# One layout of a DRAM copy, one more chunk pair in seven products, and a new order, in an attention and softplus-MLP kernel

## The chip, the cores and the metric

The kernel runs on one core of a Trainium2 chip. The metric is device microseconds of one execution; three executions of the kernel before give the median used here. One more execution was recorded by the hardware profiler, and every row shown below comes from that one.

## The reference

```python
# x: (8, 8, 512, 64) = batch B, head H, position S, D;  state: (8, 8, 32, 64)
scores = scale * np.matmul(x, state.transpose(0, 1, 3, 2))
a = softmax(scores)
xread = np.matmul(a, state)                                # (B, H, 512, 64)
scores2 = scale * np.matmul(state, x.transpose(0, 1, 3, 2))
sread = np.matmul(softmax(scores2), x)                     # (B, H, 32, 64)
attn = np.concatenate([xread, sread], axis=2)
x = attn.transpose(0, 2, 1, 3).reshape(8 * 544, 512)       # 4352 rows
h = x @ w_in                                               # 512 -> 2048
g = np.maximum(h, 0.0) + np.log1p(np.exp(-np.abs(h)))      # softplus
return (g @ w_out).astype(np.float32)                      # 2048 -> 512
```

## The kernel before, in words

Every float32 operand of a large product is held as two parts, a rounded high part and the remainder, in one double tile of 128 partitions by 2 x 512 words (4 KB a partition, 512 KB in all), and a product is three passes: high by high, high by low, low by high (`PASSES`). ScalarE writes the high part (L288), VectorE the low part (L304); `split` makes both operations.

For the positions of a batch the kernel doesn't form xread. It multiplies the states by `w_in` first: `V.{b}.{c}.{g}` holds, for batch b, column block c (four blocks of 512) and head parity g, the product of 4 heads' 32 states with their rows of `w_in`, 128 rows by 512, as high and low. The hidden block is then `h.{b}.{f} = V^T a` (L307), six wide matmuls with the softmax weights `a.{b}.{g}`, for 16 blocks f of 128. Batches 0 to 3 get their V from TensorE batch by batch (`B.V...`). Batches 4 to 7 (`STACKED`) get theirs together: for each block c, head pair q and parity o one product `B.K...` gives 128 rows by 512, the 32 states of one head for four batches (`vq`), split into `vt.{c}.{q}.{o}`. There are 32 such tiles. Each is stored to DRAM (`Sv.{c}.{q}.{o}`, the `vd` tensors, L298), and later, for each of the four batches, c and o, the load `Lv.{b}.{c}.{o}` (L295) collects the rows of that batch from the four q into one V tile. What is stored is sorted by batch, and what is loaded is sorted by head.

The second GEMM has two forms. Batches 0 to 2 use `m.{b}.{f}.{c}`, three matmuls of 512 columns each. From batch 3 on (`SWEPT`), half a batch (256 positions, two row blocks) by two blocks of the hidden dimension (u, a chunk pair: blocks 2u and 2u+1) is either a direct product of 12 matmuls of 512 columns (L756), or Strassen-like, seven products of half size, 21 matmuls of 256 columns in four steps (L746). The second form needs four sums of the softplus blocks (`sf`, L728 to L730, split into `gS`) and, once for each u, sums of the weights: `ci0.u`, `ci1.u` (L674) and `cf.u` (L680 to L683), split into `F.u`, `E` and a part of `Wc`. `SWEPT` lists the u that use it: 1 to 7 in ten half batches; (3, 0) has none; batch 8 stands for the 256 state rows.

Weights travel through DRAM too: `W.f`, 16 tiles, are stored by `Sw.f` to `wd` and come back as `Lb.f` for the second half of batch 2 and `Lc.f` from batch 3; the split `w_in` is stored by `Su` and comes back for the state rows (`Lu`). Softmax weights of the state rows pass through `te` (stores `Se`, loads `Le`).

All is placed by hand: `PLAN` is a list of `name:engine:buffers`. It sets the order on each engine, and the SBUF slot (41 double slots) or PSUM bank of each tile. Nearly every DMA is issued from SP, in the list's order; an instruction on SP waits until its data are there and its slot is free, and all behind it wait too. A slot is free when its last reader is done, and for a tile that is stored that reader is the store.

```python
V.b.c.o    = rows (q, n), q head pair, n state, of batch b      # what h reads
vt.c.q.o   = rows (b, n), of head pair q, four batches          # what is stored
```

Of the kernel before, what the change touches and what calls it, by code (L numbers as in the profile page):

```python
# [90 lines left out]
gl.2.0:V: Le.1.0.0:S: e.3.1:A: m.0.15.0:T: H.2.1:V:13 Le.1.0.2:S: gh.2.1:A:35 h.2.4:T:7 Le.1.0.1:S: H.3.1:V:1 s.2.2:A:14 Se.2.1:S: o.0.2.0:V:
Se.3.1:S: Lk.1:S:4 gl.2.1:V: m.2.0.0:T:0 So.0.0:S: m.2.0.1:T:6 s.2.3:A:12 Lk.0:S: s.2.4:A:0 m.2.0.2:T:1 gh.2.2:A:37 m.2.0.3:T:3 gh.2.3:A:8 gl.2.2:V:
B.V3.3+R1:T:2,4,5 gl.2.3:V: uh.0.3:A:22 uh.0.2:A:39 ul.0.3:V: gh.2.4:A:3 ul.0.2:V: Su.0.3:S: m.2.1.0:T: X.1:V:2 vh.3.3.0:A:23 Su.0.2:S: vh.3.3.1:A:34
m.2.1.1:T: vl.3.3.0:V: kh:A:40 vl.3.3.1:V: h.2.5:T:7 kl:V: m.2.1.2:T: s.2.5:A:3 m.2.1.3:T: B.K0.2+K0.3:T:5,2,4,7 gl.2.4:V: uh.1.0:A:27 uh.1.1:A:7
ul.1.0:V: gh.2.5:A:29 ul.1.1:V: Su.1.0:S: m.2.2.0:T: gh.v0.2.0:A:33 Su.1.1:S: gh.v0.2.1:A:17 m.2.2.1:T: gl.v0.2.0:V: gh.v0.3.0:A:25 gl.v0.2.1:V:
h.2.6:T:5 Sv.0.2.0:S: gh.v0.3.1:A:36 gl.v0.3.0:V: Sv.0.2.1:S: gl.v0.3.1:V: Sv.0.3.0:S: m.2.2.2:T: s.2.6:A:9 Sv.0.3.1:S: m.2.2.3:T:
B.K1.0+K1.1:T:2,4,7,5 gl.2.5:V: gh.2.6:A:0 m.2.3.0:T: gh.v1.0.0:A:2 gh.v1.0.1:A:13 m.2.3.1:T: gl.v1.0.0:V: gh.v1.1.0:A:35 gl.v1.0.1:V: h.2.7:T:2
Sv.1.0.0:S: gh.v1.1.1:A:22 gl.v1.1.0:V: Sv.1.0.1:S: gl.v1.1.1:V: Sv.1.1.0:S: m.2.3.2:T: s.2.7:A:14 Sv.1.1.1:S: m.2.3.3:T: gh.2.7:A:39 gl.2.6:V:
B.V3.0+V3.1:T:4,7,5,2 uh.0.0:A:28 uh.0.1:A:37 ul.0.0:V: ul.0.1:V: Su.0.0:S: Su.0.1:S: m.2.4.0:T: vh.3.0.0:A:7 vh.3.0.1:A:27 m.2.4.1:T: vl.3.0.0:V:
vh.3.1.0:A:33 vl.3.0.1:V: h.2.8:T:4 vh.3.1.1:A:17 vl.3.1.0:V: vl.3.1.1:V: m.2.4.2:T: s.2.8:A:13 gl.2.7:V: m.2.4.3:T: Lb.8:S:25 gh.2.8:A:36  # L100
B.K0.0+K0.1:T:7,5,2,4 m.2.5.0:T: gh.v0.0.0:A:4 gh.v0.0.1:A:31 m.2.5.1:T: gl.v0.0.0:V: gh.v0.1.0:A:8 gl.v0.0.1:V: h.2.9:T:7 Sv.0.0.0:S: gh.v0.1.1:A:30
Lb.9:S:6 gl.v0.1.0:V: uh.1.3:A:11 Sv.0.0.1:S: uh.1.2:A:38 gl.v0.1.1:V: Sv.0.1.0:S: m.2.5.2:T: s.2.9:A:12 ul.1.3:V: Sv.0.1.1:S: m.2.5.3:T: gh.2.9:A:2
ul.1.2:V: Su.1.3:S: T.1:T:5 h.2.10:T:2 gl.2.8:V: th.1:A: Su.1.2:S: tl.1:V: gl.2.9:V: m.2.6.0:T: s.2.10:A:1 Lb.10:S:13 m.2.6.1:T: gh.2.10:A:35
m.2.6.2:T: m.2.6.3:T: B.K1.2+K1.3:T:4,7,5,2 m.2.7.0:T: gl.2.10:V: gh.v1.2.0:A:22 gh.v1.2.1:A:3 Lb.11:S:14 m.2.7.1:T: gl.v1.2.0:V: Lz.4:S:7
gh.v1.3.0:A:28 gl.v1.2.1:V: h.2.11:T:4 Sv.1.2.0:S: gh.v1.3.1:A:37 gl.v1.3.0:V: Sv.1.2.1:S: gl.v1.3.1:V: Sv.1.3.0:S: m.2.7.2:T: s.2.11:A:8 Sv.1.3.1:S:
m.2.7.3:T: gh.2.11:A:19 M.3.0:V: h.2.12:T:7 gl.2.11:V: e.3.0:A: Ms.3.0:V: m.2.8.0:T: Lb.12:S:29 m.2.8.1:T: m.3.1:A: H.3.0:V:4 m.2.8.2:T: m.3.0:A:
N.3.1:V: Se.3.0:S: m.2.8.3:T: s.2.12:A:0 h.2.13:T:5 N.3.0:V: Nm.3.1:V: Lb.13:S:1 m.2.9.0:T: gh.2.12:A:4 s.2.13:A:3 Nm.3.0:V: m.2.9.1:T: uh.2.1:A:31
gl.2.12:V: m.2.9.2:T: uh.2.0:A:8 ul.2.1:V: gh.2.13:A:30 m.2.9.3:T: ul.2.0:V: Su.2.1:S: h.2.14:T:2 gl.2.13:V: Su.2.0:S: Lb.14:S:0 D.3.1:V:9 m.2.10.0:T:
D.3.0:V:14 s.2.14:A:2 m.2.10.1:T: gh.2.14:A:24 ah.3.1:A:11 m.2.10.2:T: ah.3.0:A:38 Lc.0:S:5 al.3.1:V: m.2.10.3:T: Lt.4.0:S:10 uh.3.0:A:21 al.3.0:V:
Lt.4.1:S:39 B.K2.0+K2.1:T:4,7,5,2 uh.3.1:A:22 Lc.1:S:3 ul.3.0:V: ul.3.1:V: Su.3.0:S: gl.2.14:V: m.2.11.0:T: Su.3.1:S: gh.v2.0.0:A:28 gh.v2.0.1:A:37  # L110
# [823 lines left out]
```

## Time and profile before

| | us |
|---|---|
| median of 3 executions (773.69 to 774.62) | 774.41 |
| the profiled execution, its own time | 775.73 |
| its span, first to last instruction | 773.9 |
| TensorE busy | 648.2 (84%) |
| VectorE busy | 448.0 (58%) |
| ScalarE busy | 365.9 (47%) |
| DMA engines, mean busy share | 0.45 |

The profiled execution's time is its span and 1.8 us around it. Names in the rows are those of the tiles with the buffer numbers left out: `vd<-vt` is a store `Sv`, `V<-vd` a load `Lv`, `wd<-W` a store `Sw`. PE is TensorE, DVE is VectorE, ACT is ScalarE, and SPq the sequencer that issues DMAs. A line that waits for several things names the one that came last. The DMA share is the mean over the core's 16 DMA engines, so 4 engines at work and 12 idle read as 0.25.

### The profile page before, as it was taken

Reading aid. Unit: us, or ns where it says so; the run is one execution under the profiler, and the core shown is the slowest. Engines: PE = TensorE matmul, PEld = TensorE weight load, DVE = VectorE, ACT = ScalarE, POOL = GpSimd, SP = SyncE. Lnnn points to the kernel's source line nnn. Section 1 sums busy time; section 2 is a strip of 40 time slices with the busy share of each in tenths; the row PEclk is TensorE's granted clock in tenths of the full one; section 3 lists DMA queues with packets and bytes.
Section 4 is the critical chain, followed back from the end, with each engine's and each line's share of the span. In section 5 each row is a group of like instructions: output and inputs, shape, how many; then the busy total and the mean of one; then the engine's idle time right before and its main releaser. Section 6 shows DMA issues by size and latency. Waiting matters only on the chain.

```text
span 773.9 us, 11435 instructions
## 1 busy us (share of the span) xinstructions
PE 648.2 (84%) x4308; PEld 537.6 (69%) x4308; DVE 448.0 (58%) x957; ACT 365.9 (47%) x729; POOL 1.0 (0%) x7
## 2 busy tenths in 40 slices
...
GB/s 354 366 83 100 178 105 65 62 266 380 128 106 187 192 164 272 167 170 122 264 195 125 227 240 110 83 116 188 95 214 148 251 148 30 139 188 118 19 28 28
DMA packets 47191, 124.22 MB, mean 161 GB/s; under 512 B 4896, under 2 KB 14624, under 8 KB 47136
## 3 DMA queue, kind: packets, MB, share of 16 engines
q1 hardware_dynamic: 46992, 122.97, 44.2%
...
q10 hardware_dynamic: 144, 0.52, 0.2%
...
## 4 chain that ended last, share of the span: by engine, by line
PE 64%; DMA 26%; DVE 5%; SPq 2%; ACT 1%; issue 1%; DVEq 0%; ACTq 0%
PE h L307 21%; DMA vd<-vt 16%; PE acc L307 12%; PE pk_X L746 6%; PE pk_Z L746 6%; PE pk_Y L746 6%; DMA Wc<-wd 4%; PE pk_Q L746 3%; DMA wd<-W 3%; PE pk_Z L756 2%; PE pk_Q L756 2%; DMA out_dram<-o 2%; PE vp L307 2%; SPq L298 1%; PE rp L307 1%
## 5 line engine op out<-in xcount | busy, mean ns | idle before, releaser
L307 PE MATMUL h<-a,V 128*128 128x512 f32 x744 | 185.1, 398 | 23.4 <-DVE vt L304 23.4
L307 PEld LDWEIGHTS h<-a,V 128*128 128x128 f32 x744 | 140.3, 192 | 54.1 <-DVE vt L304 24.7
L307 PE MATMUL acc<-W,g 128*128 128x512 f32 x480 | 120.7, 402 | 0.0
L307 PEld LDWEIGHTS acc<-W,g 128*128 128x128 f32 x480 | 91.2, 193 | 27.2 <-issue 6.6
L718 ACT ACTIVATE t<-h 128x256 f32<-128x256 f32 x156 | 51.7, 383 | 72.1 <-PE h L307 71.3
L288 ACT CAST gS<-sf 128x512 fp32r<-128x512 f32 x66 | 41.0, 622 | 58.3 <-DVE sf L730 24.4
L756 PE MATMUL pk_Z<-Wc,gA 128*128 128x512 f32 x108 | 33.6, 446 | 33.9 <-DVE gA L304 28.8
L304 DVE TENSOR_TENSOR gA<-t,gA 128x384 fp32r<-128x384 f32 (+1 forms) x78 | 44.6, 575 | 24.8 <-ACT gA L288 24.8
L304 DVE TENSOR_TENSOR gS<-sf,gS 128x512 fp32r<-128x512 f32 x66 | 44.7, 682 | 16.1 <-ACT gS L288 15.8
L288 ACT CAST gA<-t 128x384 fp32r<-128x384 f32 (+1 forms) x78 | 40.4, 535 | 27.2 <-DMA vd<-vt 8.3
L756 PEld LDWEIGHTS pk_Z<-Wc,gA 128*128 128x128 f32 x108 | 22.1, 215 | 41.5 <-DVE gA L304 30.9
L728 DVE TENSOR_TENSOR sf<-t 128x256 f32<-128x256 f32 x62 | 26.0, 419 | 38.7 <-ACT t L718 38.6
L304 DVE TENSOR_TENSOR g<-t,g 128x512 fp32r<-128x512 f32 x48 | 32.2, 685 | 27.1 <-ACT g L288 27.1
L304 DVE TENSOR_TENSOR vt<-vq,vt 128x512 fp32r<-128x512 f32 x32 | 20.4, 685 | 42.3 <-ACT vt L288 42.3
L288 ACT CAST g<-t 128x512 fp32r<-128x512 f32 x48 | 29.1, 623 | 21.2 <-DMA vd<-vt 19.6
L307 PE MATMUL acc<-Wb,g 128*128 128x512 f32 x96 | 27.6, 440 | 12.7 <-ACT u L288 12.7
L746 PE MATMUL pk_X<-Wc,gA 128*128 128x256 f32 x210 | 37.3, 286 | 0.4 <-DVE gA L304 0.4
L575 ACT ACTIVATE t<-h 128x512 f32<-128x512 f32 x48 | 27.7, 600 | 20.3 <-PE h L307 19.9
L746 PE MATMUL pk_X<-F,gS 128*128 128x256 f32 x210 | 36.6, 283 | 0.0
L746 PE MATMUL pk_Z<-Wc,gS 128*128 128x256 f32 x210 | 36.6, 283 | 0.0
L746 PE MATMUL pk_Z<-Wc,gA 128*128 128x256 f32 x210 | 36.6, 283 | 0.0
L746 PE MATMUL pk_Y<-F,gS 128*128 128x256 f32 x210 | 36.6, 283 | 0.0
...
## 6 DMA issues: line engine op xcount, KB each, us to landing
...
```

The costliest lines, as they stand in the source:

```text
L288: nc.scalar.copy(dst, src)
L298: op(name, "S", ins, list(outs), lambda e: nc.sync.dma_start(dst(), src()))
L304: lambda e: eng(e).tensor_tensor(r(dlo()), src(), dhi(), ALU.subtract))
L307: nc.tensor.matmul(dst, lhs, rhs, start=start, stop=stop)
L575: lambda e: nc.scalar.activation(at(f"t.{k}"), at(f"h.{k}"), AF.Softplus))
L718: nc.scalar.activation(dst, src.rearrange("p (c t) -> p c t", t=P), AF.Softplus)
L728: nc.vector.tensor_tensor(o[:, 0:2], a[:, 0:3:2], a[:, 3:4].broadcast_to([P, 2, P]), ALU.subtract)
L746: nc.tensor.matmul(at(bank)[:, 256 * half:256 * half + 256], r(g[:, gi, P * blk:P * blk + P]), r(wform(u, m)(wi)), start=first and pi == p ...
L756: nc.tensor.matmul(at(bank), r(page(f"gA.{k}", 2, 512)[:, gi, P * blks[i]:P * blks[i] + P]), r(page(f"Wc.{2 * u + i}", 2, DM)[:, wi]), sta ...
```

## The change

Three things are changed. **First**, a `vd` tensor holds, for each q, the 128 rows of a `vt` tile as they stand in the tile; the store is a plain copy of 128 rows. **Second**, the load of a V tile becomes four, one for each q, of the 32 rows that belong to its batch (128 loads of 128 KB in place of 32 of 512 KB), and an `h` waits for these four parts in place of the two halves. **Third**, chunk pair u = 0 joins the seven-product form in the ten half batches that use it, which adds ten `sf.*.0`, `Sh.*.0` and `Sl.*.0`, two more steps of products in each, and the weight sums of u = 0. `PLAN` is written anew with other slots and banks, and in the order that the excerpts show. Up to the 622nd of 2425 entries, which stands in the part that computes batch 2, it is the same.

```diff
-SWEPT = {(3, 0): (), (3, 1): (1, 2, 3, 4, 5, 6, 7), (4, 0): (1, 2, 3, 4, 5, 6, 7), (4, 1): (1, 2, 3, 4, 5, 6, 7), (5, 0): (1, 2, 3, 4, 5, 6, 7), (5, 1): (1, 2, 3, 4, 5, 6, 7), (6, 0): (1, 2, 3, 4, 5, 6, 7), (6, 1): (1, 2, 3, 4, 5, 6, 7), (8, 0): (1, 2, 3, 4, 5, 6, 7), (7, 0): (1, 2, 3, 4, 5, 6, 7), (7, 1): (1, 2, 3, 4, 5, 6, 7)}
+SWEPT = {(3, 0): (), (3, 1): (0, 1, 2, 3, 4, 5, 6, 7), (4, 0): (0, 1, 2, 3, 4, 5, 6, 7), (4, 1): (0, 1, 2, 3, 4, 5, 6, 7), (5, 0): (0, 1, 2, 3, 4, 5, 6, 7), (5, 1): (0, 1, 2, 3, 4, 5, 6, 7), (6, 0): (0, 1, 2, 3, 4, 5, 6, 7), (6, 1): (0, 1, 2, 3, 4, 5, 6, 7), (7, 0): (0, 1, 2, 3, 4, 5, 6, 7), (7, 1): (0, 1, 2, 3, 4, 5, 6, 7), (8, 0): (0, 1, 2, 3, 4, 5, 6, 7)}
...
-        op(f"h.{k}", "T", [f"V.{b}.{f // 4}.{g}:{x}" for g in range(2) for x in "hl"] + [f"a.{b}.{g}:{x}" for g in range(2) for x in "hl"],
+        op(f"h.{k}", "T", [f"V.{b}.{f // 4}.{g}:{x}" for g in range(2) for x in ("0123" if b in STACKED else "hl")] + [f"a.{b}.{g}:{x}" for g in range(2) for x in "hl"],
...
-                store(f"Sv.{k}.{o}", [f"vt.{k}.{o}:h", f"vt.{k}.{o}:l"],
-                      lambda c=c, q=q, o=o: io.vd[c, o].rearrange("b q n x -> q b n x")[q],
+                store(f"Sv.{k}.{o}", [f"vt.{k}.{o}:h", f"vt.{k}.{o}:l"], lambda c=c, q=q, o=o: io.vd[c, o][q],
                       lambda k=k, o=o: at(f"vt.{k}.{o}"), [f"D:vd.{c}.{o}.{q}"])
         for o in range(2):
             for b in STACKED:
-                load(f"Lv.{b}.{c}.{o}", [f"V.{b}.{c}.{o}:h", f"V.{b}.{c}.{o}:l"], lambda b=b, c=c, o=o: at(f"V.{b}.{c}.{o}"),
-                     lambda b=b, c=c, o=o: io.vd[c, o][b - STACKED[0]].rearrange("q n x -> (q n) x"), [f"D:vd.{c}.{o}.{q}" for q in range(4)])
+                for q in range(4):
+                    rows, own = slice(NS * q, NS * q + NS), slice(NS * (b - STACKED[0]), NS * (b - STACKED[0]) + NS)
+                    load(f"Lv.{b}.{c}.{o}.{q}", [f"V.{b}.{c}.{o}:{q}"], lambda b=b, c=c, o=o, rows=rows: at(f"V.{b}.{c}.{o}")[rows],
+                         lambda c=c, o=o, q=q, own=own: io.vd[c, o][q, own], [f"D:vd.{c}.{o}.{q}"])
+
 
 
     for u in sorted(set().union(*SWEPT.values())):
...
-    io.vd = {(c, o): dp.tile([len(STACKED), 4, NS, 1024], F32, tag=f"vd{c}{o}", name=f"vd{c}{o}") for c in range(4) for o in range(2)}
+    io.vd = {(c, o): dp.tile([4, P, 1024], F32, tag=f"vd{c}{o}", name=f"vd{c}{o}") for c in range(4) for o in range(2)}
```

The first five stores of `vt` tiles on SP, before (the last column is the shape of the copy as it is issued: 4 batches, 32 states, 1024 words):

```order
L298 DMA vd00_114<-vt_0_2_0_1981 4x32x1024
L298 DMA vd01_115<-vt_0_2_1_1984 4x32x1024
L298 DMA vd00_114<-vt_0_3_0_1990 4x32x1024
L298 DMA vd01_115<-vt_0_3_1_2001 4x32x1024
L298 DMA vd10_116<-vt_1_0_0_2038 4x32x1024
```

And now:

```order
L312 DMA vd00_114<-vt_0_2_0_1981 128x1024
L312 DMA vd01_115<-vt_0_2_1_1984 128x1024
L312 DMA vd00_114<-vt_0_3_0_1990 128x1024
L312 DMA vd01_115<-vt_0_3_1_2001 128x1024
L312 DMA vd10_116<-vt_1_0_0_2038 128x1024
```

The place in the queue is the same, and the shape is 128 rows.

The loads of V for blocks 1 to 3 of batch 4 on SP, before:

```order
L295 DMA xT_5_0_3377<-in_xt_dram 128x1024
L295 DMA V_4_1_0_3381<-vd10_116 128x1024
L295 DMA V_4_1_1_3414<-vd11_117 128x1024
L295 DMA V_4_2_0_3447<-vd20_118 128x1024
L295 DMA V_4_2_1_3507<-vd21_119 128x1024
L295 DMA V_4_3_0_3591<-vd30_120 128x1024
L295 DMA V_4_3_1_3605<-vd31_121 128x1024
```

And now:

```order
L309 DMA xT_5_0_3335<-in_xt_dram 128x1024
L309 DMA V_4_1_0_3395<-vd10_116 32x1024 x4
L309 DMA V_4_1_1_3435<-vd11_117 32x1024 x4
L309 DMA V_4_2_0_3597<-vd20_118 32x1024 x2
L309 DMA V_4_2_1_3609<-vd21_119 32x1024 x2
L309 DMA V_4_2_0_3597<-vd20_118 32x1024
L309 DMA V_4_2_1_3609<-vd21_119 32x1024
L309 DMA V_4_2_0_3597<-vd20_118 32x1024
L309 DMA V_4_2_1_3609<-vd21_119 32x1024
L309 DMA V_4_3_0_3658<-vd30_120 32x1024 x4
L309 DMA V_4_3_1_3726<-vd31_121 32x1024 x4
```

Six issues became 24 of a quarter the size, partly alternating between two tiles.

TensorE at the first chunk pair of the first half of batch 4 (`pk` are the banks of the result), before:

```order
L307 MATMUL h_4_5_3652<-a_4_0_3351,V_4_1_0_3381 128x512 x3
L307 MATMUL h_4_5_3652<-a_4_1_3375,V_4_1_1_3414 128x512 x3
L756 MATMUL pk_4_0_Z_3668<-Wc_0_2404,gA_4_0_0_3621 128x512 x3
L756 MATMUL pk_4_0_Z_3668<-Wc_1_2435,gA_4_0_0_3621 128x512 x3
L756 MATMUL pk_4_0_Q_3682<-Wc_0_2404,gA_4_0_0_3621 128x512 x3
L756 MATMUL pk_4_0_Q_3682<-Wc_1_2435,gA_4_0_0_3621 128x512 x3
L307 MATMUL h_4_6_3694<-a_4_0_3351,V_4_1_0_3381 128x512 x3
```

And now:

```order
L321 MATMUL h_4_7_3735<-a_4_0_3358,V_4_1_0_3395 128x512 x3
L321 MATMUL h_4_7_3735<-a_4_1_3365,V_4_1_1_3435 128x512 x3
L762 MATMUL pk_4_0_X_3750<-Wc_0_2412,gA_4_0_0_3644 128x256 x3
L762 MATMUL pk_4_0_X_3750<-F_0_2718,gS_4_0_0_3638 128x256 x3
L762 MATMUL pk_4_0_Y_3761<-Wc_0_2412,gS_4_0_0_3638 128x256 x3
L762 MATMUL pk_4_0_Y_3761<-F_0_2718,gS_4_0_0_3638 128x256 x3
L762 MATMUL pk_4_0_Z_3772<-Wc_1_2395,gA_4_0_0_3644 128x256 x3
L762 MATMUL pk_4_0_Z_3772<-Wc_1_2395,gS_4_0_0_3638 128x256 x3
L762 MATMUL pk_4_0_Q_3784<-E_0_2753,gA_4_0_0_3644 128x256 x3
L321 MATMUL h_4_8_3788<-a_4_0_3358,V_4_2_0_3597 128x512 x3
```

Twelve wide matmuls became 21 of half width, and the two hidden blocks 6 and 7 stand ahead of them in place of behind them; the hidden blocks of all swept batches move ahead by such a step.

## Rows read from the trace of the kernel before

**Rows 1.** Windows by stage: us, busy PE, PEld, DVE, ACT, POOL, clock, DMA share, GB/s

```profile
0.00:176.90 176.90, 175.00 (x1041) 129.70 (x1041) 128.84 (x252) 125.97 (x207) 1.00 (x7) 1.00 0.48 179
176.90:190.70 13.80, 0.02 (x3) 0.00 (x1) 2.50 (x4) 3.45 (x7) 0.00 (x0) 0.65 0.98 386
190.70:216.80 26.10, 26.03 (x198) 18.70 (x198) 13.59 (x23) 12.01 (x22) 0.00 (x0) 0.93 0.40 146
216.80:319.00 102.20, 59.52 (x231) 43.39 (x231) 32.20 (x54) 31.57 (x56) 0.00 (x0) 0.79 0.51 184
319.00:446.30 127.30, 65.05 (x246) 47.25 (x247) 53.05 (x114) 35.52 (x82) 0.00 (x0) 0.71 0.50 185
446.30:773.90 327.60, 322.62 (x2593) 298.60 (x2591) 217.83 (x511) 157.37 (x356) 0.00 (x0) 1.00 0.37 125
```

**Rows 2.** Waits of PE, 176.5 to 447: total us, times, longest

```profile
PE pk_Z L756 <- DVE gA L304: 28.8, 3, 18.3
PE h L307 <- DVE vt L304: 23.4, 3, 9.6
PE vq L307 <- ACT e L487: 19.4, 1, 19.4
PE rp L307 <- DMA aT<-te: 13.8, 1, 13.8
```

**Rows 3.** Chain that ended last, 190 to 440: by line, then one piece

```profile
by line: DMA vd<-vt 51.0%; DMA Wc<-wd 11.7%; DMA out_dram<-o 6.1%; PE acc L307 3.8%; SPq L298 3.4%; DMA aT<-te 2.2%; issue 2.2%; PE h L307 2.0%; PE pk_Z L756 1.8%; PE vq L307 1.7%; DVE c L674 1.3%; PE pk_Q L756 1.0%; DVE gA L304 0.9%; DVE v
...
248.89 22.79 DMA vd<-vt
```

**Rows 4.** Windows, the same columns, while one kind of store runs

```profile
165.00:176.00 11.00, 11.00 (x57) 8.85 (x63) 8.40 (x17) 9.76 (x16) 0.00 (x0) 1.00 1.00 400
201.00:234.00 33.00, 24.97 (x127) 17.22 (x126) 13.60 (x23) 13.36 (x25) 0.00 (x0) 0.84 0.27 103
```

**Rows 5.** SP timeline: start us, us, what it issues

```profile
161.70 17.21 SPq L298 DMA_DIRECT2D wd<-W  x16
...
262.62 16.10 SPq L298 DMA_DIRECT2D vd<-vt  x4
```

**Rows 6.** Groups on PE, 190.7 to 446.3, first, fifth and sixth

```profile
L307 PE MATMUL h<-a,V 128*128 128x512 f32 x162 | 44.2, 422 | 23.4 <-DVE vt L304 23.4
...
L756 PE MATMUL pk_Q<-Wc,gA 128*128 128x512 f32 x54 | 17.0, 460 | 0.0
L307 PE MATMUL vq<-u,K 64*128 64x512 f32 x96 | 16.5, 460 | 21.7 <-ACT e L487 19.4 <-DVE V L304 1.7 <-DVE vt L304 0.5
```

**Rows 7.** PE timeline, one direct and one seven-product pair: start us, us

```profile
476.84 1.52 PE L756 MATMUL pk_Z<-Wc,gA 128*128 128x512 f32 x6
...
479.56 2.88 PE L307 MATMUL h<-a,V 128*128 128x512 f32 x12
482.28 0.52 PE L746 MATMUL pk_X<-Wc,gA 128*128 128x256 f32 x3
...
484.79 2.91 PE L307 MATMUL h<-a,V 128*128 128x512 f32 x12
```

**Rows 8.** Groups on DVE, whole run, by form

```profile
L304 DVE TENSOR_TENSOR gS<-sf,gS 128x512 fp32r<-128x512 f32 x66 | 44.7, 682 | 16.1 <-ACT gS L288 15.8 <-issue 0.3
...
L728 DVE TENSOR_TENSOR sf<-t 128x256 f32<-128x256 f32 x62 | 26.0, 419 | 38.7 <-ACT t L718 38.6
...
L674 DVE TENSOR_TENSOR c<-Wc 128x512 f32<-128x512 f32 x9 | 6.1, 681 | 45.4 <-DMA out_dram<-o 23.2 <-DMA Wc<-wd 22.2
```

**Rows 9.** Windows, the same columns: eight small stores; a dense stretch

```profile
713.90:718.60 4.70, 4.70 (x22) 3.90 (x21) 3.32 (x7) 2.04 (x6) 0.00 (x0) 1.00 0.41 112
500.00:520.00 20.00, 20.00 (x147) 19.02 (x147) 19.35 (x47) 12.27 (x28) 0.00 (x0) 1.00 0.38 126
```

**Rows 10.** The `vd` tile's issues on SP: ns least, median, most

```profile
L298 SPq DMA_DIRECT2D vd<-vt x32: 508/3156/10980, 200.2 to 387.4; - x32
L295 SPq DMA_DIRECT2D V<-vd x32: 319/326/1433, 430.0 to 707.0; - x32
```

More of the change, by code (lines that the diff above doesn't have):

```diff
@@ L91 @@
[L91 to L110, printed above, removed]
@@ new lines @@
+h.2.6:T:2 Sv.0.2.0:S: gh.v0.3.1:A:36 gl.v0.3.0:V: Sv.0.2.1:S: gl.v0.3.1:V: Sv.0.3.0:S: m.2.2.2:T: s.2.6:A:9 Sv.0.3.1:S: m.2.2.3:T:
+B.K1.0+K1.1:T:0,4,7,2 gl.2.5:V: gh.2.6:A:0 m.2.3.0:T: gh.v1.0.0:A:2 gh.v1.0.1:A:8 m.2.3.1:T: gl.v1.0.0:V: gh.v1.1.0:A:13 gl.v1.0.1:V: h.2.7:T:0
+Sv.1.0.0:S: gh.v1.1.1:A:39 gl.v1.1.0:V: Sv.1.0.1:S: gl.v1.1.1:V: Sv.1.1.0:S: m.2.3.2:T: s.2.7:A:14 Sv.1.1.1:S: m.2.3.3:T: gh.2.7:A:40 gl.2.6:V:
+B.V3.0+V3.1:T:4,7,2,0 uh.0.0:A:27 uh.0.1:A:28 ul.0.0:V: Lb.8:S:7 ul.0.1:V: Su.0.0:S: Su.0.1:S: m.2.4.0:T: vh.3.0.0:A:9 vh.3.0.1:A:23 m.2.4.1:T:
@@ new lines @@
+sf.4.0.3:V:0 p.4.0.0.3:T:2 h.4.8:T:6 gh.4.0.2:A:29 Sh.4.0.3:A:38 gl.4.0.2:V: h.4.9:T:0 s.4.0.4.0:A:8 s.4.1.4.0:A:82 gh.4.0.3:A:8 p.4.0.1.0:T:
+s.4.0.4.1:A: Sl.4.0.2:V: s.4.1.4.1:A: p.4.0.1.1:T: gl.4.0.3:V: p.4.0.1.2:T: sf.4.0.4:V:4 p.4.0.1.3:T: h.4.10:T:5 Sh.4.0.4:A:10 gh.4.0.4:A:23
+gl.4.0.4:V: h.4.11:T:3 s.4.0.5.0:A:9 s.4.1.5.0:A:3 p.4.0.2.0:T: s.4.0.5.1:A: Sl.4.0.3:V: s.4.1.5.1:A: p.4.0.2.1:T: gh.4.0.5:A:4 sf.4.0.5:V:10
+p.4.0.2.2:T: gl.4.0.5:V: Sh.4.0.5:A:6 p.4.0.2.3:T: M.5.0:V: T.4:T:6 h.4.12:T:0 th.4:A: M.5.1:V: e.5.0:A: tl.4:V: Ms.5.0:V: h.4.13:T:5 Ms.5.1:V:
@@ new lines @@
+Sh.4.1.6:A:4 Le.5.1.2:S: gh.4.1.7:A:23 Le.5.1.3:S: h.5.1:T:4 gl.4.1.7:V: s.5.0.0.0:A:0 sf.4.1.7:V:7 s.5.1.0.0:A:8 p.4.1.4.0:T: s.5.0.0.1:A:
+Sl.4.1.5:V: s.5.1.0.1:A: p.4.1.4.1:T: p.4.1.4.2:T: p.4.1.4.3:T: h.5.2:T:7 Sh.4.1.7:A:33 Lt.6.1:S:34 h.5.3:T:2 sf.5.0.0:V:1 s.5.0.1.0:A:12
+s.5.1.1.0:A:2 p.4.1.5.0:T: s.5.0.1.1:A: Lx.5.1:S:25 Sl.4.1.6:V: s.5.1.1.1:A: Lx.5.0:S:29 p.4.1.5.1:T: p.4.1.5.2:T: p.4.1.5.3:T: h.5.4:T:1
+Sh.5.0.0:A:38 Lt.6.0:S:39 Sl.4.1.7:V: sf.5.0.1:V:6 h.5.5:T:4 s.5.0.2.0:A:3 s.5.1.2.0:A:9 p.4.1.6.0:T: s.5.0.2.1:A: s.5.1.2.1:A: p.4.1.6.1:T:
@@ new lines @@
+Lv.6.1.1.0:S:5 Lv.6.1.1.1:S: al.6.1:V: Lv.6.1.1.2:S: p.5.1.3.0:T: A.7.0:V:2 qk.7.0:A:5 Lv.6.1.1.3:S: qk.7.1:A:7 A.7.1:V:9 p.5.1.3.1:T: X.6:A:4
+E.7.0:V: p.5.1.3.2:T: Sh.5.1.4:A:8 gh.5.1.4:A:10 E.7.1:V: p.5.1.3.3:T: Sh.5.1.5:A:34 h.6.0:T:5 Sl.5.1.4:V: gh.5.1.5:A:39 gh.5.1.6:A:29 gl.5.1.4:V:
+gh.5.1.7:A:38 h.6.1:T:1 gl.5.1.5:V: s.6.0.0.0:A:11 sf.5.1.6:V:1 s.6.1.0.0:A:8 gl.5.1.6:V: p.5.1.4.0:T: s.6.0.0.1:A: Sl.5.1.5:V: s.6.1.0.1:A:
+Lx.7.1:S:33 p.5.1.4.1:T: M.7.0:V: p.5.1.4.2:T: M.7.1:V: e.7.0:A: p.5.1.4.3:T: sf.5.1.7:V:0 h.6.2:T:4 Lx.7.0:S:8 gl.5.1.7:V: Lv.6.2.0.0:S:10
@@ new lines @@
+Sh.6.0.3:A:8 r.7.0:V: Lv.6.3.1.3:S: r.7.1:V: gh.6.0.3:A:33 p.6.0.1.1:T: X.7:V:6 gl.6.0.3:V: p.6.0.1.2:T: Lu.0.3:S:25 p.6.0.1.3:T: h.6.8:T:2
+Lu.0.2:S:17 Sl.6.0.2:V: Lu.0.0:S:29 h.6.9:T:4 s.6.0.4.0:A:4 s.6.1.4.0:A:7 h.6.10:T:5 s.6.0.4.1:A: s.6.1.4.1:A: sf.6.0.4:V:5 h.6.11:T:3 s.6.0.5.0:A:13
+s.6.1.5.0:A:1 p.6.0.2.0:T: s.6.0.5.1:A: Lu.0.1:S:10 Sl.6.0.3:V: s.6.1.5.1:A: Lu.1.0:S:38 p.6.0.2.1:T: sf.6.0.5:V:11 p.6.0.2.2:T: p.6.0.2.3:T:
+h.6.12:T:2 Sh.6.0.4:A:6 Lu.1.1:S:34 h.6.13:T:4 s.6.0.6.0:A:10 s.6.1.6.0:A:3 p.6.0.3.0:T: s.6.0.6.1:A: Sl.6.0.4:V: s.6.1.6.1:A: p.6.0.3.1:T:
@@ new lines @@
+gh.6.1.0:A:6 sf.6.1.3:V:10 Sh.6.1.1:A:39 p.6.0.7.1:T: gl.6.1.0:V: p.6.0.7.2:T: Sl.6.1.1:V: p.6.0.7.3:T: sf.6.1.4:V:24 p.6.1.0.0:T:4 e1.6.0:A:5
+gh.6.1.1:A:8 e2.6.0:V: p.6.1.0.1:T:5 e3.6.0:V: p.6.1.0.2:T:3 gl.6.1.1:V: e4.6.0:V: p.6.1.0.3:T:2 e5.6.0:V: p.6.1.1.0:T: Sh.6.1.2:A:6 e6.6.0:V:
+So.6.0.0:S: gh.6.1.2:A:23 p.6.1.1.1:T: Sl.6.1.2:V: So.6.0.1:S: p.6.1.1.2:T: gl.6.1.2:V: sf.6.1.5:V:6 p.6.1.1.3:T: p.6.1.2.0:T: Sh.6.1.3:A:8
+gh.6.1.3:A:39 p.6.1.2.1:T: Sl.6.1.3:V: p.6.1.2.2:T: gl.6.1.3:V: p.6.1.2.3:T: p.6.1.3.0:T: Sh.6.1.4:A:6 Lu.1.2:S:23 gh.6.1.4:A:5 p.6.1.3.1:T:
```

274 lines of the change are left out of this document (142 added, 132 removed).

## The prediction

> **What bounds the kernel now.** I read the windows by stage first [rows 1]. Up to 176.9 us TensorE is busy 175.0 us, and from 446.3 us on 322.6 of 327.6 us at full clock: both ends are bound by TensorE. The 269.4 us between are not. There TensorE waits 13.8 us, then works without a gap for 26.1 us, then is busy 59.5 of 102.2 and 65.1 of 127.3 us, at a mean granted clock of 0.79 and 0.71, so it also works part of that time at the lower of its two levels. No other engine is full either: VectorE has 53.1 us in the last of these windows, and the DMA engines a share of 0.50.
>
> Its waits [rows 2] name VectorE and ScalarE as releasers, for tiles of all kinds, which says that these engines wait themselves. So I went to the chain [rows 3]: from 190 to 440 us 51% of it are stores of `vt` tiles, some 128 us, and one such store takes 22.8 us from issue to landing for 512 KB. The reason is in two windows [rows 4]. While `wd<-W` is stored the DMA share is 1.00 at 400 GB/s. While only `vd<-vt` stores run it is 0.27 at 103 GB/s, that is four engines of sixteen (0.25). Both move whole tiles of 512 KB from 128 partitions in rows of 4 KB; they differ in the shape in DRAM, 128x1024 against 4x32x1024 (the first two excerpts of the order). SP shows the same [rows 5]: 16 `wd` stores are accepted in 17.2 us, 1.1 us each, and four `vd` stores in 16.1 us, 4.0 us each, up to 11.0 us [rows 10]. Everything else also uses those four engines, so every load and store that is queued behind a `vd` store waits for it, and with it the slots. 32 stores at 512 KB / 103 GB/s = 5.1 us are 163 us on the four engines, on top of their share of the other traffic.
>
> **The stores (first edit).** Now of the shape of the `wd` stores, a store should take 512 KB / 400 GB/s = 1.3 us of all sixteen, 42 us for 32, spread. The waits that go are those of [rows 2] without the one of 13.8 us: the three rows give 71.6 of the 42.7 + 62.2 = 105 us in which TensorE is not busy in the last two windows of the middle [rows 1]. What is late next, from 190.7 to 446.3 us? Three floors. DMA: the shares give 0.40 x 26.1 + 0.51 x 102.2 + 0.50 x 127.3 = 10.4 + 52.1 + 63.7 = 126 us of all sixteen engines; the same bytes stay. TensorE: 450 wide matmuls in five groups, the first and the last shown [rows 6], at 2.72 us for 12 when the clock is full [rows 7] = 102 us, the 96 of `vq` at most 16.5, together about 119 without a few small groups. VectorE: 98.8 us [rows 1] and what the third edit adds. So the stretch takes 126 us at the least in place of 255.6, if all overlaps. It won't: 126, 119 and 105 us of work with dependences in between. The only price in the trace for a burst of transfers that TensorE has to wait for is the 13.8 us behind the 16 `wd` stores [rows 1, 2]; that wait stands ahead of the stretch and stays, since those stores keep their place. The new order has a second burst of the kind, where the first half of batch 3 begins: six `Lc` loads and the last four `Sv` stores in a row, about 13 us of all engines, ahead of weight sums on VectorE that read them. I take one more such wait and round it to 15: 126 + 15 = 141 us.
>
> **The loads (second edit).** 96 more issues on SP. One issue of a V load takes 0.33 us in the median, 1.4 at most [rows 10], so 128 take 42 us of SP's time, nearly all of it after 446 us, in 327 us; behind them on SP stand the loads of x, the `te` traffic and the output stores, which have slack of that size between batches. The nearest row to a transfer of 32 rows: eight stores of 64 KB were issued from 713.9 us on and their bytes moved in a window of 4.7 us [rows 9], 0.6 us each, share 0.41, so more than four engines work on them. I take 0, since TensorE runs through 20 us windows there with nothing idle [rows 9]; bounds 0 and +10 us.
>
> [...]
>
> **The third edit.** A direct pair takes 479.56 - 476.84 = 2.72 us of TensorE, seven products 484.79 - 482.28 = 2.51 [rows 7]: 0.2 us less, ten times, 2.0 us, nine of them in the stretch where TensorE is the bound. For it VectorE gets in each half batch one `sf`, a first part of 0.42 us and two of half the size, so 1.3 at most, and a low part of 0.68 [rows 8]: ten times 2.0 = 20 us; and for u = 0 once two sums of 0.68 and seven pieces of at most 0.68, at most 6.1 us. ScalarE gets the casts that go with them. The cover: after 446.3 us VectorE is busy 217.8 of 327.6 us. The densest window has 19.35 of 20 us with TensorE still full [rows 9], so a few us could come through there; I take 0, bounds 0 and +6. The 6.1 us fall where batch 3 begins and are in the 15 above.
>
> **The order (PLAN).** Up to the middle of batch 2 it is the same; then slots change, and the hidden blocks of swept batches stand one step earlier on TensorE (third excerpt). No instruction is removed by that; it gives VectorE and ScalarE a step more of lead, in a stage without waits. 0, bounds -2 and +2.
>
> **Sum.** 190.7 (unchanged) + 141 + 327.6 - 2.0 = 657.3 us of span in place of 773.9. The profiled execution's time was 1.8 above its span and 1.3 above the median: 657.3 + 1.8 - 1.3 = 658 us.
>
> **Rivals.**
> *Bursts don't overlap.* The wait moves to the transfers: TensorE needs data for half of its work in the stretch while they are in flight. 126 + 119 / 2 = 186 us, so 703 us. For it: the loads `Lc` already make 11.7% of the chain [rows 3], and SP issues in order. Against it: 26.1 us of gapless work at a share of 0.40 [rows 1], right after the first burst.
> *The burst ahead shrinks too.* The order of the 16 `wd` stores is new, so the 13.8 us may go, and the stretch may reach its floor: 176.9 + 126 + 325.6 + 0.5 = 629 us; anything below 643 I count here. Against it: still 16 stores at 1.1 us ahead of what TensorE waits for.
> *The change doesn't do what it says:* the stores stay on four engines, for a reason other than the shape. Then the stretch keeps its 255.6 us, TensorE gains 2.0 and VectorE adds up to 6 where it is waited for: 772 to 778 us. Against it: the `wd` stores in the same form have a share of 1.00 [rows 4]. [...]
> *Slower: the loads become the bound.* The 32 loads of a batch must land in the time of one batch, about 325 / 4.5 = 72 us. From t = 72 / 32 = 2.25 us for a load, one after another, TensorE begins to wait; from (72 + 116 / 4) / 32 = 3.2 us the whole gain is gone, and at 4 us the time is 658 + 4 x (128 - 72) = 882 us. The row has 0.6 us [rows 9], and SP's most is 1.4 us [rows 10].
>
> **How the numbers follow.** Forecast (643 to 675 us) 0.60; bursts (675 to 725) 0.20; below 643 0.08; a smaller gain still (725 to 770), from waits that the stores cover now, 0.05; stores on four engines 0.04, half of it no change and half slower; loads 0.03. Faster 0.93, same 0.02, slower 0.05, where 0.2% (1.5 us) is about what a measurement of this kernel can tell from no change. The range: 643 less the -2 of the order, and upward to where the rest of the bursts leaves two in ten outside: 641 to 698 us.
>
> **What would show it.** After: the DMA share near 1.00 in windows with `vd<-vt` alone, landing in a few us; SP's median issue for it near 1 us; `B.R1`'s wait of some 14 us still at 177 us; the first seven-product pair of batch 3 at about 190.7 + 141 = 332 us in place of 446; the stretch after it as long as before, less 2 us, without waits for `V`. If TensorE waits for `Wc` sums or for transfers at the start of batch 3 for over 30 us, the bursts have it; if it waits for `V`, the loads. If the stretch stays over 200 us with the stores on sixteen engines, slots were not the link, and this reading is wrong.

## The result, and the profile after

The changed kernel takes 654.13 us (median of 4 runs, 653.96 to 656.15) where the kernel before takes 774.51 us (773.69 to 775.43, 4 runs on the same chip): a ratio of 0.8451, 95% interval 0.8432 to 0.847. Its profiled execution took 654.07 us, 2.2 us more than its span of 651.9. (In the changed kernel the line numbers are some 15 higher: `h` matmuls are L321, stores L312, loads L309, the seven products L762, direct pairs L772.)

The windows by stage, to be held against [rows 1]. Each row has the window, its length, then busy time and count of PE, PEld, DVE, ACT and POOL, the granted clock, the DMA share and GB/s. I cut at 323.1 us, where the pair u = 0 of batch 3 ends; in the kernel before the same pair ends at 446.3 us.

```profile
0.00:176.90 176.90, 175.02 (x1041) 129.73 (x1041) 129.45 (x254) 127.22 (x210) 1.00 (x7) 1.00 0.48 180
176.90:190.70 13.80, 0.24 (x12) 0.27 (x16) 1.48 (x3) 2.00 (x4) 0.00 (x0) 0.64 0.98 384
190.70:323.10 132.40, 126.24 (x684) 96.56 (x676) 97.01 (x190) 78.34 (x162) 0.00 (x0) 0.97 0.91 347
323.10:651.90 328.80, 321.11 (x2674) 301.09 (x2673) 232.79 (x560) 161.54 (x369) 0.00 (x0) 1.00 0.41 125
```

The first two rows are those of before. All of the gain lies in the third: 255.6 us have become 132.4. It has two parts. TensorE was not busy for 255.6 - 150.6 = 105.0 us of it and is now for 6.2: 98.8 us. And what it does takes 126.2 us in place of 150.6, for 684 matmuls in place of 675: 24.4 us. The granted clock of the stretch is 0.97, and it was 0.77, as one row over the same stretch of the kernel before shows:

```profile
190.70:446.30 255.60, 150.60 (x675) 109.33 (x676) 98.83 (x191) 79.10 (x160) 0.00 (x0) 0.77 0.49 180
```

I put the 24.4 us down to it: 150.6 x 0.77 = 116 and 126.2 x 0.97 = 122, so in terms of a full clock the work is about the same. By this reading a fifth of the gain is paid by the clock, which is at the higher of its two levels for nearly all of the stretch once the gaps are gone: in windows of 2 us from 176 us on the kernel before reads 1.00 or 0.50, with a value between only where it changes, and the changed kernel reads under 1.00 in its stretch only up to 196 us and from 316 to 322 us. The last row is 1.2 us longer than its counterpart of 327.6.

The waits of TensorE, whole run: releaser, total us, times, longest. They answer to [rows 2].

```profile
PE rp L321 <- DMA aT<-te: 13.7, 1, 13.7
PE pk_Z L772 <- ACT gA L302: 2.4, 1, 2.4
PE h L321 <- ACT t L734: 2.4, 1, 2.4
PE pk_X L762 <- DVE rs L481: 1.6, 1, 1.6
PE pk_X L762 <- DVE gA L318: 1.5, 1, 1.5
PE pk_Z L772 <- DVE gA L318: 1.4, 2, 0.9
```

The wait behind the 16 `wd` stores is there as before (13.7, was 13.8); the long waits for `gA`, `vt` and `e` are gone. The rows for L772 and the one for `h` are in the stretch (6.2 us together), those for L762 in the last part. The chain of work that ended last, by engine and by line, which had 51% of 190 to 440 us in `vd<-vt` [rows 3]:

```profile
PE 77%; DVE 10%; DMA 7%; SPq 3%; issue 1%; ACT 1%; DVEq 0%; ACTq 0%
PE h L321 25%; PE acc L321 19%; PE pk_X L762 8%; PE pk_Z L762 7%; PE pk_Y L762 7%; PE pk_Q L762 4%; PE vp L321 2%; SPq L312 2%; PE vq L321 2%; DMA aT<-te 2%; DMA wd<-W 2%; DVE gA L318 1%; DMA Wc<-wd 1%; DMA out_dram<-o 1%; PE sc L321 1%
```

No transfer of `vd` is left in it. Next a window in which only `vd<-vt` stores are issued (the counterpart of the second row of [rows 4]), the same stores and the `wd` stores on SP's timeline (start us, us, what), and the `vd` tile's issues (ns least, median, most; first and last start):

```profile
201.00:208.00 7.00, 7.00 (x37) 5.27 (x36) 4.18 (x8) 3.27 (x6) 0.00 (x0) 1.00 1.01 410
```

```profile
161.53 17.36 SPq L312 DMA_DIRECT2D wd<-W  x16
...
200.00 8.66 SPq L312 DMA_DIRECT2D vd<-vt  x8
```

```profile
L309 SPq DMA_DIRECT2D V<-vd x128: 302/419/1494, 309.5 to 589.3; - x128
L312 SPq DMA_DIRECT2D vd<-vt x32: 319/320/1484, 200.0 to 283.7; - x32
```

All sixteen engines carry the stores (share 1.01 at 410 GB/s, was 0.27 at 103), SP hands them over at 1.1 us each as it does the `wd` stores, and the longest issue takes 1.5 us in place of 11.0. Nobody waits for a load of `V`, though there are 128 now.

### The profile page after: what moved, and what is told of

Its sections match the earlier page's. It is cut to its first block, busy times and chain, and to the rows that moved or that the text cites. A ratio compares the mean times of both kernels' runs of the same rounds, so it can differ in the third digit from the quotient of the medians.

```text
span 651.9 us, 11867 instructions
## 1 busy us (share of the span) xinstructions
PE 622.6 (95%) x4398; PEld 527.6 (81%) x4398; DVE 460.7 (71%) x1005; ACT 369.1 (57%) x743; POOL 1.0 (0%) x7
## 4 chain that ended last, share of the span: by engine, by line
PE 77%; DVE 10%; DMA 7%; SPq 3%; issue 1%; ACT 1%; DVEq 0%; ACTq 0%
PE h L321 25%; PE acc L321 19%; PE pk_X L762 8%; PE pk_Z L762 7%; PE pk_Y L762 7%; PE pk_Q L762 4%; PE vp L321 2%; SPq L312 2%; PE vq L321 2%; DMA aT<-te 2%; DMA wd<-W 2%; DVE gA L318 1%; DMA Wc<-wd 1%; DMA out_dram<-o 1%; PE sc L321 1%
## 5 line engine op out<-in xcount | busy, mean ns | idle before, releaser
L321 PE MATMUL h<-a,V 128*128 128x512 f32 x744 | 180.7, 391 | 2.4 <-ACT t L734 2.4
L321 PEld LDWEIGHTS h<-a,V 128*128 128x128 f32 x744 | 137.4, 188 | 31.2 <-ACT t L734 2.8
L321 PE MATMUL acc<-W,g 128*128 128x512 f32 x480 | 118.8, 397 | 0.0
L321 PEld LDWEIGHTS acc<-W,g 128*128 128x128 f32 x480 | 89.7, 189 | 26.1 <-issue 6.3
L762 PE MATMUL pk_X<-Wc,gA 128*128 128x256 f32 x240 | 43.3, 288 | 3.1 <-DVE rs L481 1.6
L762 PEld LDWEIGHTS pk_X<-Wc,gA 128*128 128x128 f32 x240 | 36.8, 191 | 6.7 <-DVE gA L318 3.7
L762 PE MATMUL pk_Z<-Wc,gS 128*128 128x256 f32 x240 | 41.8, 283 | 0.0
L762 PE MATMUL pk_Z<-Wc,gA 128*128 128x256 f32 x240 | 41.8, 283 | 0.0
L762 PE MATMUL pk_Y<-F,gS 128*128 128x256 f32 x240 | 41.8, 283 | 0.0
L762 PE MATMUL pk_Y<-Wc,gS 128*128 128x256 f32 x240 | 41.8, 283 | 0.0
L762 PE MATMUL pk_Q<-E,gA 128*128 128x256 f32 x240 | 41.8, 283 | 0.0
L762 PE MATMUL pk_X<-F,gS 128*128 128x256 f32 x240 | 41.8, 283 | 0.0
L762 PEld LDWEIGHTS pk_Z<-Wc,gA 128*128 128x128 f32 x240 | 34.6, 192 | 0.0
L762 PEld LDWEIGHTS pk_Q<-E,gA 128*128 128x128 f32 x240 | 34.6, 192 | 0.0
```

Source lines behind the costliest of these rows:

```text
L321: nc.tensor.matmul(dst, lhs, rhs, start=start, stop=stop)
L762: nc.tensor.matmul(at(bank)[:, 256 * half:256 * half + 256], r(g[:, gi, P * blk:P * blk + P]), r(wform(u, m)(wi)), start=first and pi == p ...
```

## Experiments

Each kernel was timed against the kernel before on the same chip. The first five ask what made the stores faster and which of the three edits earned the gain, the sixth and seventh look at the loads and at u = 0, the last two at the wait that is left.

**1. The layout alone.** The kernel before, with the new layout of `vd` and the four loads for each V tile; order and u = 0 as before.

```
-  vd tile [len(STACKED), 4, NS, 1024]
+  vd tile [4, P, 1024]
-  store to io.vd[c, o].rearrange("b q n x -> q b n x")[q]
+  store to io.vd[c, o][q]
+  V loaded by four copies of 32 rows, io.vd[c, o][q, own]
```

> The kernel before with the new DRAM layout of the stacked products and the loads in four, and nothing else: old order, old slots, chunk pair 0 direct. Theory (the stores took four DMA engines, all else followed): 650 to 665 us, the stretch from 190 us to the first seven-product pair of batch 3 at some 130 us, the DMA share there near 0.9. Rival (the new order is what fills the stretch, the layout only helps): over 700 us.

Measured: 657.4 us (656.14 to 658.67), ratio 0.849 (0.8475 to 0.8504). The windows up to the first seven-product pair, which starts at 329.23 us, and behind it:

```profile
190.70:329.23 138.53, 130.24 (x673) 99.00 (x664) 97.29 (x189) 77.89 (x160) 0.00 (x0) 0.94 0.87 332
329.23:656.00 326.77, 322.62 (x2593) 298.58 (x2591) 218.00 (x513) 157.53 (x356) 0.00 (x0) 1.00 0.40 126
```

Time and DMA share (0.87) are as expected; the stretch is 8.5 us longer than the 130 us that I named. The layout with its loads earns 117 of the 120 us. Order and u = 0 together are worth 3.3.

**2. Stores by batch again.** The changed kernel, with the layout in DRAM and the stores' shape of before (4x32x1024), all else new.

```
-  vd tile [4, P, 1024];  store to io.vd[c, o][q]
+  vd tile [len(STACKED), 4, NS, 1024];  store to io.vd[c, o].rearrange("b q n x -> q b n x")[q]
```

> The kernel after with the stores as before, sorted by batch, in the shape 4x32x1024; the loads stay in four parts of 32 rows, the order and the seven products stay new. Theory: back to 765 to 790 us, with a DMA share near 0.26 while only these stores run. Rival (the new order makes up for slow stores): below 700 us.

**3. The shape without the places.** Rows lie as in the changed kernel, but with one empty row behind each 32, so that a store must keep the form 4x32x1024.

```
-  vd tile [4, P, 1024];  store to io.vd[c, o][q]
+  vd tile [4, 4, NS + 1, 1024];  store to io.vd[c, o][q, :, 0:NS]
```

> The kernel after, with a row left empty behind each 32 rows of the DRAM tensors, so that a store has to be issued as 4x32x1024 again while its rows lie nearly together; loads, order and products stay new. Theory (four engines because the slowest dimension is 4): 765 to 790 us, DMA share near 0.26 while only these stores run. Rival (the places in DRAM): 654 us.

**4. Two in place of four.** As experiment 2, each store issued as two copies of 2x32x1024.

```
-  store to io.vd[c, o].rearrange("b q n x -> q b n x")[q]
+  two stores to io.vd[c, o].rearrange("b q n x -> q b n x")[q, 2 * i:2 * i + 2]
```

> The kernel after with the stores sorted by batch, each as two copies 2x32x1024. Theory (a copy takes as many engines as its slowest dimension, and the fullest engines set the stretch): the same two engines carry all stores, 512 KB over two engines at 25.8 GB/s each (103 GB/s over four before) is 10.2 us, 32 of them 326 us, with the other traffic of some 84 us a stretch of about 410 us in place of 130: 900 to 950 us. Rival (the time is set by something that the stores only delay): not above 790 us.

Measured: 770.34, 770.93 and 930.48 us (one run each; spans 768.2, 768.8 and 928.3), each within what was expected. A window of each while `vd` stores run, in this order:

```profile
201.00:234.00 33.00, 26.68 (x129) 18.39 (x129) 12.77 (x21) 12.58 (x23) 0.00 (x0) 0.84 0.27 98
```

```profile
201.00:234.00 33.00, 26.66 (x129) 18.46 (x128) 12.72 (x21) 12.58 (x23) 0.00 (x0) 0.84 0.27 99
```

```profile
215.00:270.00 55.00, 21.57 (x69) 14.60 (x67) 7.71 (x13) 7.16 (x14) 0.00 (x0) 0.63 0.13 53
```

Four groups give a share of 0.27 whether the groups lie 512 KB apart or with one row between them; two groups give 0.13, half of it. So for these stores it is the number at the front of the copy's shape in DRAM that sets the number of engines (128: share 1.01, 4: 0.27, 2: 0.13), not where the bytes go, and the order of the plan can't make up for it. The tile's side has 128 rows in the first two cases and 64 in experiment 4, so it doesn't account for the step from 1.01 to 0.27.

Nor do copies that are in flight together spread over more engines here. In experiment 4 SP hands over 16 of them, 4 MB, in 66.5 us; at 53 GB/s these bytes take 79 us, so several are under way at a time, and the share is still 0.13:

```profile
199.63 66.49 SPq L313 DMA_DIRECT2D vd<-vt  x16
```

**5. The old places, stores in four.** The kernel before; each store as four copies of 32x1024 to the places it had. The loads stay whole.

```
-  one store to io.vd[c, o].rearrange("b q n x -> q b n x")[q]
+  four stores of 32 rows to io.vd[c, o][i, q]
```

> The kernel before, with the same DRAM layout and the same bytes to the same places, but each store as four copies of 32 rows (32x1024); loads in one as before. Theory (what counts is the shape of the copy as it is issued, not where the rows go): 655 to 675 us; 96 more issues on SP in the busy stretch, at some 0.4 us each 38 us of SP's time, may cost up to 15. Rival (rows scattered over DRAM are slow to write): as before, 765 to 780 us.

Measured: 679.26 us (677.19 to 680.8), ratio 0.877 (0.8747 to 0.8793), over the upper end that I gave. SP's timeline for the first eight stores, and TensorE's longest waits:

```profile
200.73 16.33 SPq L306 DMA_DIRECT2D vd<-vt  x32
```

```profile
PE rp L315 <- DMA aT<-te: 13.8, 1, 13.8
PE vq L315 <- ACT e L495: 10.5, 1, 10.5
PE pk_Z L764 <- DVE gA L312: 4.9, 2, 4.6
PE pk_Z L764 <- ACT gA L296: 4.7, 1, 4.7
```

Now more than four engines are in use, and 95 us of the gain are there. A window in which only these copies are issued, the whole stretch up to the first seven-product pair, and VectorE's longest wait for a load in it:

```profile
201.00:217.00 16.00, 16.00 (x101) 11.14 (x101) 9.53 (x16) 9.25 (x17) 0.00 (x0) 1.00 0.90 280
```

```profile
190.70:349.77 159.07, 134.82 (x675) 100.56 (x668) 97.55 (x189) 78.52 (x160) 0.00 (x0) 0.90 0.85 289
```

```profile
DVE c L682 <- DMA Wc<-wd: 13.1, 2, 12.7
```

The stretch is 20.5 us longer than in experiment 1, and two things became dearer. SP is occupied for 16.3 us by eight tiles in place of 8.7, 0.5 us for each of 32 issues. And the copies of 32 rows take more of the engines: a share of 0.90 moves 280 GB/s, where the stores of 128 rows moved 410 at 1.01. Over the stretch that is 0.85 x 159.07 = 135 us of all engines, against 0.87 x 138.53 = 121 in experiment 1 for the same 46.0 MB (289 x 159.07 and 332 x 138.53). The loads that batch 3 begins with come later: VectorE waits 12.7 us for one of `Wc`, and 10.5 us of TensorE's time go into the wait for `e`, which needs a transpose that VectorE makes only after that wait. The changed kernel pays the same 96 issues as loads in the last part, where SP and the engines (share 0.41) have the time. Which of the two, SP or the engines, sets the pace here isn't shown; neither was varied by itself.

**6. One load of the new layout.** The changed kernel, V loaded by a single copy whose source is 4x32x1024.

```
-  four loads of io.vd[c, o][q, own] into 32 rows each
+  one load of io.vd[c, o][:, own] into the tile
```

> The kernel after with each V tile loaded by one copy of 512 KB whose source has the shape 4x32x1024, in place of four of 32 rows. If the smaller of the two sides counts, the loads run on four engines, 5.1 us each, eight of them 41 us in a batch of some 72 us: hidden, 654 to 665 us, with the DMA share near 0.25 where only loads run. If only the destination's 128 partitions count, the share is near 1 and the time 654.

Measured: 681.17 us (679.36 to 682.14), ratio 0.8784 (0.8767 to 0.8802): 27 us slower than the changed kernel, and over both of the times that I expected. The first seven-product pair starts at 320.42 us, as in the changed kernel (320.28), so the loss is all behind it. The last part, and TensorE's longest waits in it:

```profile
326.30:680.00 353.70, 328.64 (x2544) 304.56 (x2543) 235.52 (x567) 161.93 (x371) 0.00 (x0) 0.97 0.34 117
```

```profile
PE h L309 <- DMA V<-vd: 11.6, 3, 4.5
PE h L309 <- ACT t L719: 3.9, 2, 2.8
PE pk_X L747 <- DVE gS L306: 3.8, 2, 3.0
```

Against the changed kernel's row for the part from 326.3 us on (325.70 us, of them 317.91 busy) TensorE is idle 25.1 us in place of 7.8 and busy 10.7 us longer for the same work, at a granted clock of 0.97 in place of 1.00: 28 us together. So the loads have to leave in four pieces: the shape binds a load as it binds a store, even where the mean DMA share is only 0.34. The last eight loads run alone (SP's timeline, then a window):

```profile
584.46 29.98 SPq L297 DMA_DIRECT2D V<-vd  x8
```

```profile
587.00:614.00 27.00, 27.00 (x207) 26.02 (x206) 15.17 (x33) 11.90 (x29) 0.00 (x0) 1.00 0.26 105
```

It is four engines again, 0.26 at 105 GB/s, as I expected for this shape. What I had wrong is that 41 us of loads would hide in a batch of 72 us.

**7. u = 0 direct.** The changed kernel with the first chunk pair of each half batch computed by the direct pair, as before.

```
-  SWEPT = {..., (3, 1): (0, 1, 2, 3, 4, 5, 6, 7), ...}
+  SWEPT = {..., (3, 1): (1, 2, 3, 4, 5, 6, 7), ...}
```

> The kernel after with chunk pair 0 as a direct product again in all half batches, without its sums of weights and of softplus blocks; layout, loads, order and slots stay new. By the prediction's term (0.2 us of TensorE for each of ten pairs) 2.0 us slower than the changed kernel; by the trace after, where TensorE waits 1.6 and 1.5 us for VectorE at the start of batch 4, between 1 us faster and 1 us slower.

Measured: 654.53 us (654.08 to 656.44), ratio 0.8446 (0.8431 to 0.8462), against 654.13: no difference that can be measured, as the trace of the changed kernel had suggested, and not the 2.0 us of the prediction. Its direct pair u = 0 of batch 3 ends at 321.0 us, and behind it TensorE waits for VectorE (timeline, then waits from 318 us on):

```profile
319.57 1.52 PE L765 MATMUL pk_Q<-Wc,gA 128*128 128x512 f32 x6
321.02 0.65 PE L314 MATMUL rp<-x,aT 128*32 128x64 f32 x32
```

```profile
PE pk_X L755 <- DVE gA L311: 3.4, 4, 1.6
PE pk_X L755 <- DVE gS L311: 1.1, 1, 1.1
```

**8. The awaited loads ahead.** From here on the question is the wait of 13.7 us. The changed kernel, with the three loads of `aT` that the first product behind the wait needs (they read `te`) moved ahead of the 16 `wd` stores, and the two loads of `ks` right behind these.

```
-  Sw.13 ... Sw.4 So.0.2 Se.2.0 Le.1.0.2 Le.1.0.0 Le.1.0.1 Se.2.1 Se.3.1 Lk.0 So.0.0 Lk.1
+  Le.1.0.2 Le.1.0.0 Le.1.0.1 Sw.13 ... Sw.4 Lk.0 Lk.1 So.0.2 Se.2.0 Se.2.1 Se.3.1 So.0.0
```

> The kernel after with three small loads of the state rows' softmax weights (batch 1) issued ahead of the sixteen stores of W in place of behind them, and the two loads of the stacked states right behind those. Theory (the 13.7 us wait is only the place in the queue): the wait for these loads goes, the next is the product of the stacked states, which needs its operands about 187 us: 8 to 12 us faster, 642 to 647 us. Rival (the stretch behind it is bound by the DMA engines, share 0.91, so it gives the time back): 651 to 655 us.

**9. `ks` ahead too.** The kernel of experiment 8, with `ks` in a tile slot that is free early, and its loads also ahead of the stores.

```
-  Le.1.0.1 Sw.13 ... Sw.4 Lk.0:S:4 Lk.1 ... H.3.1:V:1
+  Le.1.0.1 Lk.0:S:1 Lk.1 Sw.13 ... Sw.4 ... H.3.1:V:4
```

> The kernel with three te stores ahead of the burst of 16 wd stores (648.56 us), and now the two ks loads (the stacked state, 256 KB in all) ahead of that burst too, in another tile slot. Theory A, TensorE's wait is what sets the end: the wait of TensorE that was left, 7.5 us for the rounded copy of ks at 189.5 us, goes, and the first seven-product pair starts some 5 to 7.5 us earlier (306 to 308 in place of 313.3); time 641 to 644. Theory B, the transfers set the end of this stretch: their share of the 16 DMA engines was 0.99 from 160 to 190 us and 0.97 from 190 to 313.3, so only some 0.01 x 30 + 0.03 x 123 = 4.0 us of engine time is idle there, and no order of the same transfers can bring the first pair forward by more; the wait comes back as waits on later loads or stores, the pair starts at 310 to 313.3; time 645.5 to 648.6.

(The three transfers that this text calls `te` stores are the loads of `aT` from `te`.)

Measured: experiment 8 648.56 us (648.32 to 648.98), ratio 0.8367 (0.8355 to 0.8378), experiment 9 647.0 us (646.78 to 647.98), ratio 0.8355 (0.8344 to 0.8367). Both beat the changed kernel, by 5.6 and 7.1 us, and both give less than the 13.7; between the two the intervals of the ratios overlap. For experiment 8 neither of the two expected times was met: the gain is less than 8 us, and more than the rival allowed. TensorE's longest wait in the one:

```profile
PE vq L319 <- ACT K L300: 7.5, 1, 7.5
```

and in the other, with ScalarE's own wait from 170 to 200 us, and the stretch of the stores and the one behind it:

```profile
PE h L319 <- DVE vt L316: 5.7, 1, 5.7
```

```profile
ACT g L300 <- DMA out_dram<-po: 6.3, 1, 6.3
```

```profile
160.00:190.00 30.00, 25.06 (x190) 18.83 (x182) 18.82 (x35) 19.88 (x37) 0.00 (x0) 0.97 1.00 388
190.00:313.32 123.32, 116.86 (x574) 89.23 (x575) 90.10 (x176) 74.96 (x156) 0.00 (x0) 0.96 0.97 367
```

Each time the wait passes to the next thing that stands behind the burst: first the `aT` loads, then the `ks` loads (ScalarE rounds them before a product can use them), then a store of `po`, whose tile ScalarE wants for its next `g`. The share of the engines is 1.00 over these 30 us, so something has to come late. The first seven-product pair starts at 320.28, 313.32 and 312.05 us: it comes forward by 7.0 and 8.2 us, about what the wait shrank by (6.2 and 8.0), and by the spans (651.9, 646.5 and 645.0 us) 1.3 to 1.6 of that is lost behind it. In experiment 9 the theory that TensorE's wait alone sets the end asked for a pair at 306 to 308 us and a time of 641 to 644; the one by transfers, 310 to 313.3 and 645.5 to 648.6, held. Whether the 30 us could be filled by moving part of the 16 stores themselves wasn't tried.

## Why the prediction came out as it did

The forecast of 658 us, range 641 to 698, held: 654.13. The mechanism held too. That the sum came so near is in part luck: the stretch was put 8.6 us too long and the part behind it 3.2 too short. Point by point:

*The stores, and the shape as the cause:* shown. The new form runs at 410 GB/s on all sixteen engines, the old form falls back to 0.27 with the new plan around it (experiments 2 and 3), and splitting the store in its old places brings most of the gain back (5). The rival that the stores stay on four engines is out.

*The wait ahead of the stretch stays:* right, 13.7 us. The SP issue of a `vd` store is 0.32 us in the median, not near 1; it is 1.1 only within a burst of eight.

*The stretch, 141 us:* measured 132.4 for the same work. 126 came from the DMA floor and 15 from one more burst that TensorE would have to wait for. Three errors lie in it. The engines' work, for the same bytes, is 0.91 x 132.4 = 120 us and not 126. It is TensorE that fills the stretch, with 126.2 us busy where I counted 119; that this equals the 126 of the sum is chance. I put the difference to the granted clock of 0.97, where I had reckoned with full, and to the small groups that I left out. And the second burst, six `Lc` loads and four stores, costs no 15 us: the waits in the stretch are 2.4 + 2.4 + 1.4 = 6.2. The first seven-product pair, for which I gave 332 us, started at 320.28 (first row of the timeline below); it is u = 0 now, one pair earlier than I had in mind, and u = 1 started at 325.19.

*The order, 0 within -2 and +2, and u = 0, -2.0:* both were mis-sized, and experiments 1 and 7 take them apart. From 190.7 us to the end of the pair u = 0 in batch 3, and from there to the end of the span:

| kernel | stretch, us | last part, us | span, us |
|---|---|---|---|
| before | 255.6 | 327.6 | 773.9 |
| layout alone (1) | 138.5 | 327.7 | 656.9 |
| and the new order (7) | 130.3 | 332.6 | 653.6 |
| and u = 0 in seven products (changed) | 132.4 | 328.8 | 651.9 |

The layout alone gives 138.5 and 327.7, where the sum had 141 for the stretch, u = 0 included, and 327.6 for the part behind it. The order (with its slots) takes 8.2 us out of the stretch and gives 4.9 back in the last part, where TensorE waits 3.4 + 1.1 us for VectorE, 0.4 in the kernel before. The seven products for u = 0 cost 2.1 us in the stretch, where VectorE gets its extra pieces, and take 3.8 out of the last part. These are single executions; by the medians the order is worth 2.9 us, beyond the 2 that I gave as its bound, and u = 0 is worth 0.4, which is inside the spread of the runs, so a gain of 2.0 isn't shown. That VectorE's extra work for u = 0 would cost nothing is what failed: I had put the weight sums into the 15 us of a burst that didn't come. In the changed kernel the last part was to be 325.6 and is 328.8. TensorE is busy for 1.5 us less in it than before (321.1, was 322.6), but idle for 7.7 us in place of 5.0; its two waits for VectorE are 1.6 and 1.5 us, here the first of them in batch 4 (timeline of TensorE, the released matmul in the last row):

```profile
320.28 0.78 PE L762 MATMUL pk_X<-Wc,gA 128*128 128x256 f32 x3
...
325.19 0.62 PE L762 MATMUL pk_X<-Wc,gA 128*128 128x256 f32 x3
...
335.69 0.40 PE L762 MATMUL pk_X<-Wc,gA 128*128 128x256 f32 x2
337.66 0.38 PE L762 MATMUL pk_X<-Wc,gA 128*128 128x256 f32 x1 [1.58 <-DVE rs L481]
```

Together: 8.6 us too much in the stretch, to its end at 190.7 + 141 = 331.7, and 3.2 too little behind it, hence 651.9 of span and not 657.3.

*The loads, 0 within 0 and +10:* right. Their issue is 0.42 us in the median, not 0.33, and a load lands in 3.1 us; nobody waits for one. Thirty-two loads in four pieces each are free where thirty-two whole ones of the wrong shape cost 27 us (6), so the rival in which the loads bind was nearer than its 0.03 suggests, but by shape and not by number. The engines do pay for the split: with the layout alone their work behind the stretch is 0.40 x 326.8 = 131 us, and before it was 0.37 x 327.6 = 121 for the same bytes, but at such shares that stays beside other work: the last part takes 327.7 us with the layout alone and its 96 more loads, and 327.6 before.

*Bursts don't overlap (703):* out, the waits in the stretch are 6.2 us. *The burst ahead shrinks (629):* its condition, the awaited loads ahead of the 16 stores, is that of experiments 8 and 9, and the time is 647.0 and not 629. In experiment 9 the pair u = 0 of batch 3 ends at 314.7 us where this rival has 176.9 + 126 = 302.9, because other loads and stores queue behind the same 16 stores; and the part behind it takes 330.4 us where it has 325.6.
